# Weight loads moved to the opening and row loads moved back in a fused attention and GLU kernel

## The chip, the core and the metric

The kernel runs on one core of a Trainium2 chip. A core has five instruction streams: TensorE (PE, matrix products; its weight loads are listed as PEld), VectorE (DVE), ScalarE (ACT), GpSimd (POOL) and SyncE (SP, which here only issues transfers). The streams run side by side, each in its own order, and wait for one another through semaphores. The metric is the device time of one execution in microseconds; the time of a kernel is the median of several runs.

## The reference

The program computes a transformer block with adaptive normalisation. A vector c gives six rows of scales and shifts. The first half is attention with a memory, over 2048 tokens in four segments of 512, 32 heads of width 16; the second half is a bilinear GLU.

```python
mod = (silu(c) @ w_mod).reshape(1, 6, 1, -1)
sa, ca, ga, sb, cb, gb = (mod[:, i] for i in range(6))
h = layernorm(x) * (1 + ca) + sa
q, k, v = h @ wq, h @ wk, h @ wv          # 32 heads of 16, 4 segments of 512
for s in range(4):
    p = softmax(qs @ ks.T * scale + mask)  # within the segment
    a_dot = p @ vs
    a_mem = (phi(qs) @ M) / (phi(qs) @ z + 1e-6)
    o = g * a_mem + (1 - g) * a_dot        # g = sigmoid(beta)
    M, z = M + phi(ks).T @ vs, z + phi(ks).sum(0)
x = x + ga * (o @ wo)
h = layernorm(x) * (1 + cb) + sb
x = x + gb * (((h @ w_gate) * (h @ w_up)) @ w_down)
```

phi(t) is t + 1 where t > 0 and exp(t) elsewhere; the mask of the source keeps, for each query, the keys at or after it.

## The kernel before, in words

Heads are worked on in four groups of eight (g = 0 to 3), tokens in segments (s = 0 to 3). Each matrix product in full precision is three products of split operands: high times high, low times high, high times low. A raw weight block is loaded, ACT copies it into the high part, and POOL (or DVE) subtracts to get the low part.

**Opening (L1099 to L1142).** `load_g` (L708) is a generator of two steps: the first takes a staging buffer from the list `stage` (L700) in the order of the calls and issues the load of one group's weights on SP; the second makes ACT's copy (L722) and the subtraction (L723). Weights of groups 0, 1 and 2 are loaded by the opening itself, in that order (`w1`, `w2`); those of group 3 only in `fill_a` (L1003 to L1006), when group 2 begins, with the second step between the keys and the queries of group 2 (L1028). The staging list gives k0, q0 and the first value block the buffers `ph`, then the value blocks `mem`, `pkr`, `f`, then `x` four times, then `mem` twice.

**Projections (`a_kq`, L769).** The keys or the queries of one group and segment are twelve products into one PSUM bank: four blocks of 128 rows of the normalised input (high part `ahH`, low part `ahL`), each in the three forms. For the first keys of segments 1 to 3 a sort (L778) puts all products with `ahH` first and the four with `ahL` behind. ACT copies the bank out (`kf`, `qf`), ACT and POOL split it into three bf16 parts, and SP writes these to DRAM (`kd`, `qd`), from where `load` (L271) brings them into `kst` and `qst`.

**The loop of scores (L1145 to L1203).** It runs over 32 units u, four heads each; u = 8s + 2g + j. In `q_step` PE makes scores by query and DVE takes the row maxima (`nm`); `n_step` transposes those, and a transfer on ACT's queue puts them into two more rows of `qst`. In `k_step` PE makes scores by key and ACT takes the exponential (`pt`), POOL masks it (L341); `av_step` multiplies by v, ACT copies the result (`tsb`) and issues its write `td` on its own queue (L369). Between these steps `fill` draws work from two generators, `fill_a` (projections, memory) and `fill_b` (output projection, the second normalisation, the first gate weights). A number that each step yields decides how much is drawn.

**The tail of the loop (`fill_b`, L1044).** Rows of finished attention output (`orl`) are loaded per segment. Those of segment 2 are loaded when a flag `o0` is set and three segments are done (L1191). `weave(a, b, at)` (L687) puts steps of b at given positions between steps of a; with it the output projection of segment 1 (`wo_mm`) is mixed with `lnC(0)`, which loads the four row blocks `x1_0` of segment 0 and normalises them on DVE, and with `prep(0)` (L435), which loads the first gate and up weights (`w0`), combines them on POOL (L457) and splits them (L448, L452).

**Order of issue.** The rows below show each engine's order as the program fixes it. Every transfer signals on one of eight completion lanes, DMAHW0 to DMAHW7, taken in turn by all transfers of SP and ACT. A transfer waits, before it is issued, until the one that used its lane last has landed; its own lane is the first that its row names. So a transfer issued by ACT can hold ACT for a load that ACT does not need.

Of the kernel before, what the change touches and what calls it, by code (L numbers as in the profile page):

```python
# [20 lines left out]
KT = D // P  # L21
# [37 lines left out]
def tile_kernel(ctx, tc, x, wq, wk_, wv, wo, beta, w_gate, w_up, w_down, c, w_mod, out):  # L59
# [29 lines left out]
    def MM(*a, **k):  # L89
        return pe(nc.tensor.matmul(*a, **k))  # L90
# [19 lines left out]
    def bank(name, dt=F32, shape=(P, 512)):  # L110

        nbank[0] += 1
        return pst(shape, btag[nbank[0] % len(btag)], name, dt)
# [49 lines left out]
    def give():  # L163
        while kept:
            kept.pop(0)()
# [521 lines left out]
    def weave(a, b, at):  # L687

        i = 0
        for w in a:  # L690
            yield w
            if w:
                for _ in range(at.count(i)):
                    w = next(b, None)
                    if w or w is False:
                        yield w
                i += 1

    wH, wL = {}, {}
    stage = [("ph", 3), ("ph", 3), ("ph", 3), ("mem", 2), ("pkr", 1), ("f", 2)] + [("x", 4)] * 4 + [("mem", 2)] * 2  # L700
    nst = [0]

    def staged(nm):
# [65 lines left out]
    def a_kq(s, g, nm):  # L769

        hH, hL = hcur[0]
        ph = phs.setdefault((s, g), {})
        if True:
            dst = kd if nm == "k" else qd
            ps = bank(f"{nm}ps{s}_{g}")
            terms = [(k, a, b) for k in range(KT) for a, b in ((wH, hH), (wL, hH), (wH, hL))]
            if s > 0 and g == 0 and nm == "k":
                terms.sort(key=lambda t: t[2] is hL)  # L778
            for n, (k, a, b) in enumerate(terms):
                MM(ps, a[nm, g][:, k, :], b[k], start=n == 0, stop=n == 11)  # L780
                if n in (2, 5, 8):
                    yield 0.68
            give()
            f = pa.tile([P, L], F32, tag="f", name=f"{nm}f{s}_{g}", bufs=2)
            fast = s == 0 and g == 0
            A, V = (CA, CV) if fast else (act, nc.gpsimd)
            A.activation(f, ps, AF.Copy)
            q3 = pa.tile([P, 3, L], BF, tag="q3", name=f"{nm}3_{s}_{g}", bufs=2)
            r = pa.tile([P, L], F32, tag="qr", name=f"{nm}r_{s}_{g}", bufs=2)

            def part0():
                behind(A.activation(q3[:, 0, :], f, AF.Copy))
                V.tensor_sub(r, f, q3[:, 0, :])

            if fast:
                part0()
            else:
                keep(part0)

            def rest():  # L800
                (CV.tensor_copy if fast else act.copy)(q3[:, 1, :], r)
                V.tensor_sub(q3[:, 2, :], r, q3[:, 1, :])
                for r0, n, k in ((0, 3, 0), (3, 2, 0), (5, 1, 0)) if nm == "k" else ((0, 1, 3), (3, 1, 2), (5, 1, 1)):
                    if nm == "k":
                        nc.sync.dma_start(dst[s][g][r0:r0 + n].rearrange("r p t -> p r t"), q3[:, 0:n, :])
                    else:
                        i = 3 - k
                        nc.sync.dma_start(dst[s][g][r0:r0 + k].rearrange("r p t -> p r t"),
                                          q3[:, i:i + 1, :].to_broadcast([P, k, L]))

            if fast:
                rest()
            phi = (nm == "k" and s < NSEG - 1) or (nm == "q" and s > 0)
            if phi:
                if fast:
                    yield 0.0
                phlog.append((s, g, nm))
                while memq and (s == NSEG - 1 and g > 0 or len(phlog) > 3 and phlog[-4] not in phdone):
                    yield mem_step() or 0.0
                e = pa.tile([P, L], F32, tag="ph", name=f"ph{nm}{s}_{g}", bufs=3)  # L820
                rl = pa.tile([P, L], F32, tag="rl", name=f"rl{nm}{s}_{g}", bufs=1)

                def phi0():
                    behind(act.activation(rl, f, AF.Relu))
                    behind(act.activation(e, f, AF.Exp))

                if fast:
                    phi0()
                else:
                    keep(phi0)  # L830
                ph[nm] = e
            yield 0.68
            if not fast:
                give()
                rest()
            if phi:
                later.append([lambda: pin(vec.scalar_tensor_tensor(e, e, 1.0, rl, op0=ALU.min, op1=ALU.add)), 0, nm])
                if fast:
                    flush("kq")
        nkq[s, g] = nkq.get((s, g), 0) + 1  # L840
        if nkq[s, g] == 2:
            done.add((s, g))
# [97 lines left out]
    B = {"h0": []}  # L940
# [46 lines left out]
    def fill_a():  # L987
# [5 lines left out]
        for s in range(NSEG):  # L993
# [5 lines left out]
            for g in range(2 if s == 0 else 0, NG):  # L999
                ws = []  # L1000
                if s == 0 and g == 2:
                    xts[1] = xload(1)
                if s == 0 and g < 3:  # L1003
                    ws = [load_g(nm, w, g + 1) for nm, w in (("k", wk_), ("q", wq))]
                for w in ws:
                    next(w)  # L1006
                K, Q = a_kq(s, g, "k"), a_kq(s, g, "q")
                if s == 0 and g == 2:
                    lns = a_ln(1)
# [2 lines left out]
                if s < 3 and g > 0:  # L1012
                    p, q = (STEPS0 if s == 0 else STEPS)[g]
# [30 lines left out]
    def fill_b():  # L1044
        open_b()
        pb, bc = B["pb"], B["bc"]
        o1 = wo_load(1, pb, (0, 1))
        xr0 = xr_load(0, pb, (2,))
        o1 += wo_load(1, pb, (2, 3))
        rest = wo_mm(0, us[0], xr0 + xr_load(0, pb, (3,)), (2, 3))  # L1050
        pr = prep(0, "0_0", bc, 1, pb, 1)
        op = wo_op(1, pb, o1, us[1])
        yield from weave(rest, op, (4, 5, 6, 7))
        B["o0"] = True
        lg = lnC(0, pb, bc, pb, "x1", 4)
        rest = weave(wo_mm(1, us[1], xr_load(1, pb, (0,)), pb=pb), chain(op, islice(lg, 10)),
                     (0, 1, 4, 5, 6, 7, 8, 11, 12, 13, 14))
        yield from weave(rest, islice(pr, 1), (10,))
        while "o2" not in B:
            yield None  # L1060
        yield from weave(kept_as("nxt", lg), wo_op(2, pb, B["o2"], us[2]), (0, 1, 2, 3, 3))
        B["orl_free"] = True
        lg = lnC(1, pb, bc, pb, "x1", 4)
        rest = weave(wo_mm(2, us[2], xr_load(2, pb, (0,)), pb=pb), lg, (0, 3, 4, 5, 6, 7, 10, 11, 12, 13))
        yield from weave(rest, pr, (1, 8, 9, 14))
        B["hf"] = yield from lg

    def kept_as(nm, g):
        B[nm] = yield from g
# [47 lines left out]
        pass  # L1117
    next(lw[2])
    next(lw[2])
    w1 = [load_g(nm, w, 1) for nm, w in (("k", wk_), ("q", wq))]  # L1120
    for w in w1:
        next(w)
    run(kq0[1])
    run(kq0[0])
# [111 lines left out]
    hH, hL = B["nxt"]  # L1236
# [94 lines left out]
    for q in range(2):  # L1331
# [62 lines left out]
        for i in range(NF):  # L1394
            g = pre.pop(i + 2) if i + 2 < NF else iter(())
            if i == 0:
                g = chain(pre.pop(1), g)
# [32 lines left out]
        for m in range(2):  # L1430
            s = 2 * q + m
# [111 lines left out]
```

## Time and profile before

| what | us |
|---|---|
| median of 3 runs | 868.59 (866.88 to 870.31) |
| the profiled execution | 865.84 |
| its span on the core | 864.0 |
| opening and first half of the loop, 0 to 430 | 430 |
| end of the loop, 430 to 535 | 105 |
| GLU, 535 to 864 | 329 |

The profile was taken in one execution, and its stamps count from the start of its span. A row of a timeline gives the start, the busy time, the engine, the source line, the operation with output and input, and in brackets how long the engine stood still before it and what ended that. A row of the chain of waits gives start, length and what the end of the program was then waiting for. DMA is the share of the sixteen DMA engines that is busy.

### The profile page before, as it was taken

How to read it: one execution, taken by the hardware profiler on the slowest of the kernel's cores; microseconds unless marked ns; L12 is line 12 of the kernel's file. 1: busy time of each engine (PE TensorE's matmuls, PEld its weight loads, DVE VectorE, ACT ScalarE, POOL GpSimd, SP SyncE). 2: the span in 40 equal slices, each digit the busy share in tenths (PEclk: the TensorE clock that was granted, in tenths of full speed). 3: DMA queues.
4: the chain of work that ended last, by engine and by line, in shares of the span. 5: the costliest groups of instructions: out<-in, count | busy, mean ns of one | idle time of the engine just before them, and what ended most of it. 6: DMA issues, size and time to landing. Idle time of an engine off the chain costs nothing.

```text
span 864.0 us, 14347 instructions
## 1 busy us (share of the span) xinstructions
PE 827.9 (96%) x4823; PEld 580.5 (67%) x4824; DVE 652.1 (75%) x1730; ACT 473.7 (55%) x740; POOL 422.7 (49%) x562
## 2 busy tenths in 40 slices
PE   8979999999999999989997999999999999999998
PEld 5746566556665566555654567888778888887886
DVE  8688678988779777789898878888785667667532
ACT  3747867698668875577545663333364333323321
POOL 4535744577346753586314806998101855550000
PEclk9999999999999999999999999999999999999999
DMA  7773748477566655967894453563315241122032
GB/s 244 233 199 123 229 154 229 151 251 245 159 200 207 214 187 167 271 221 215 253 280 158 148 171 114 168 182 117 107 31 168 74 123 49 50 56 95 0 119 98
DMA packets 111355, 139.45 MB, mean 161 GB/s; under 512 B 18800, under 2 KB 70000, under 8 KB 111280
## 3 DMA queue, kind: packets, MB, share of 16 engines
q1 hardware_dynamic: 106016, 130.91, 49.4%
q10 hardware_dynamic: 5264, 7.62, 2.4%
q8 instruction: 38, 0.62, 0.3%
q14 instruction: 37, 0.30, 0.1%
HBM read 87.48 MB, written 50.76 MB: 160 GB/s over the span
## 4 chain that ended last, share of the span: by engine, by line
PE 70%; DMA 8%; DVE 8%; ACT 6%; POOL 5%; issue 3%; SPq 1%; ACTq 0%; POOLq 0%; DVEq 0%
PE g L90 24%; PE acc L90 14%; PE tb L90 6%; PE k L90 5%; PE q L90 5%; PE vps L90 4%; DVE q L40 3%; PE wops L90 3%; PE kps L90 3%; PE qps L90 3%; ACT pt L338 2%; DMA qd<-q 1%; DMA orl<-od 1%; DMA qst<-nt 1%; DMA memb<-memd 1%
## 5 line engine op out<-in xcount | busy, mean ns | idle before, releaser
L40 DVE CUSTOM_DVE_ANT_0 q<-q,cmask 128x384 f32<-128x384 f32 (+3 forms) x512 | 246.7, 508 | 56.2 <-PE q L90 46.1
L338 ACT ACTIVATE pt<-k 128x1024 f32<-128x1024 f32 x160 | 163.9, 1025 | 66.7 <-PE k L90 54.7
L341 POOL TENSOR_SCALAR_AFFINE_SELECT pt<-pt 128x256 f32<-128x256 f32 (+1 forms) x224 | 106.3, 488 | 143.5 <-ACT pt L338 138.9
L90 PE MATMUL q<-kst,qst 96*128 96x384 bf16 (+3 forms) x512 | 101.3, 300 | 8.4 <-DVE nm L40 7.4
L90 PE MATMUL k<-qst,kst 98*128 98x384 bf16 (+3 forms) x512 | 97.5, 302 | 7.8 <-ACT pt L338 7.3
L457 POOL TENSOR_TENSOR w<-w 128x256 f32<-128x256 f32 (+1 forms) x84 | 72.5, 875 | 65.9 <-DVE t L1228 37.9
L452 POOL TENSOR_TENSOR AL<-w,AH 128x512 fp32r<-128x512 f32 (+1 forms) x42 | 58.8, 1403 | 46.4 <-ACT AH L448 46.4
L90 PE MATMUL tb<-pt,v 128*32 128x512 f32 (+3 forms) x1024 | 75.7, 436 | 0.6 <-POOL pt L341 0.6
L90 PEld LDWEIGHTS <-kst 98*128 98x128 bf16 x512 | 38.2, 99 | 53.1 <-issue 46.0
L40 DVE DVE_READ_ACCUMULATOR2_ANT nm<- 128x1 f32 x512 | 72.1, 141 | 0.0
L448 ACT ACTIVATE AH<-w 128x512 fp32r<-128x512 f32 (+3 forms) x88 | 47.3, 565 | 43.3 <-POOL w L457 30.1
L90 PEld LDWEIGHTS <-qst 96*128 96x128 bf16 x512 | 43.4, 98 | 36.4 <-issue 11.6
L1485 DVE TENSOR_TENSOR mL<-mid,mH 128x512 fp32r<-128x512 f32 (+1 forms) x44 | 32.3, 738 | 41.5 <-ACT mH L1484 41.5
L90 PE MATMUL acc<-DH,mL 128*128 128x512 f32 x144 | 56.6, 393 | 0.9 <-DVE mL L1485 0.9
L90 PE MATMUL acc<-DH,mH 128*128 128x512 f32 x144 | 57.1, 397 | 0.0
L90 PE MATMUL acc<-DL,mH 128*128 128x512 f32 x144 | 56.5, 393 | 0.0
L1484 ACT ACTIVATE mH<-mid 128x512 fp32r<-128x512 f32 (+1 forms) x44 | 27.1, 627 | 51.7 <-PE acc L90 50.5
L90 PEld LDWEIGHTS tb<-pt,v 128*32 128x32 f32 x1024 | 28.6, 109 | 39.3 <-issue 34.5
L1277 ACT ACTIVATE p<-g 128x512 f32<-128x512 f32 (+1 forms) x22 | 13.1, 597 | 74.3 <-PE g L90 74.3
L452 DVE TENSOR_TENSOR AL<-w,AH 128x512 fp32r<-128x512 f32 (+3 forms) x44 | 32.6, 743 | 14.0 <-ACT AH L448 13.9
L367 ACT ACTIVATE tsb<-tb 128x512 f32<-128x512 f32 x32 | 19.1, 596 | 31.8 <-PE tb L90 31.7
L90 PE MATMUL g<-chH,AH 128*128 128x512 f32 (+1 forms) x88 | 34.8, 395 | 0.7 <-ACT p L1277 0.7
(286 smaller groups left out, 2054.6 us busy)
## 6 DMA issues: line engine op xcount, KB each, us to landing
kst<-kd SPq DMA_DIRECT2D x32, 384.0 KB
qst<-qd SPq DMA_DIRECT2D x32, 384.0 KB
td<-tsb ACTq DMA_DIRECT2D x28, 256.0 KB
wm<-in_w_mod_dram SPq DMA_DIRECT2D x24, 256.0 KB
kd<-k SPq DMA_DIRECT2D x16, 384.0 KB
qd<-q SPq DMA_DIRECT2D x16, 384.0 KB
w<-in_w_gate_dram SPq DMA_DIRECT2D x20, 256.0 KB
w<-in_w_up_dram SPq DMA_DIRECT2D x40, 128.0 KB
```

Of the source, the lines that this page charges most:

```text
L40: i = getattr(self.eng, name)(*a, **k)
L90: return pe(nc.tensor.matmul(*a, **k))
L338: lpt[0] = act.activation(pt, kp, AF.Exp, scale=0.25)
L341: sels[u, i] = nc.gpsimd.affine_select(w, w, pattern=[[0, w.shape[1]], [1, P]], compare_op=ALU.is_ge, fill=0.0, base=0, channel_multiplier=-1)
L367: act.activation(tsbs[u], tbs.pop(u), AF.Copy)
L448: i = act.activation(hi[sl], w[sl], AF.Copy)
L452: i = eng.tensor_sub(lo[sl], w[sl], hi[sl].bitcast(F32))
L457: i = ce.tensor_tensor(w[:, o, :, 0:n], w[:, x, :, 0:n], w[:, y, :, 0:n], op=op)
L1277: lcp[0] = act.activation(r["p1"], ps, AF.Copy)
L1484: pin(act.activation(mH[0:n], md[0:n], AF.Copy))
L1485: vec.tensor_sub(mL[0:n], md[0:n], mH[0:n].bitcast(F32))
```

## The change

Four edits. The loads of group 3's raw weights are issued in the opening, right behind those of group 1; their split stays between group 2's keys and queries. The staging list is reordered so that each of them keeps the buffer that it had. The sort of the first keys of segments 1 to 3 now keeps the fourth block's three products together at the end. In `fill_b` the flag `o0` is set later, from a step inside the output projection of segment 1, the steps of `lnC(0)` come up to one position earlier, and the first step of `prep(0)` moves from position 10 to 14; in segment 2's projection one step of `prep(0)` moves from position 1 to 4.

```diff
-    stage = [("ph", 3), ("ph", 3), ("ph", 3), ("mem", 2), ("pkr", 1), ("f", 2)] + [("x", 4)] * 4 + [("mem", 2)] * 2
+    stage = [("ph", 3), ("ph", 3), ("ph", 3), ("mem", 2), ("pkr", 1), ("f", 2)] + [("x", 4)] * 2 + [("mem", 2)] * 2 + [("x", 4)] * 2
...
             if s > 0 and g == 0 and nm == "k":
-                terms.sort(key=lambda t: t[2] is hL)
+                terms.sort(key=lambda t: (t[0] == KT - 1, t[2] is hL))
...
                 if s == 0 and g == 2:
                     xts[1] = xload(1)
-                if s == 0 and g < 3:
-                    ws = [load_g(nm, w, g + 1) for nm, w in (("k", wk_), ("q", wq))]
-                for w in ws:
-                    next(w)
+                    ws = w3
...
         yield from weave(rest, op, (4, 5, 6, 7))
-        B["o0"] = True
         lg = lnC(0, pb, bc, pb, "x1", 4)
         rest = weave(wo_mm(1, us[1], xr_load(1, pb, (0,)), pb=pb), chain(op, islice(lg, 10)),
-                     (0, 1, 4, 5, 6, 7, 8, 11, 12, 13, 14))
-        yield from weave(rest, islice(pr, 1), (10,))
+                     (0, 1, 4, 5, 6, 7, 7, 10, 11, 12, 13))
+        yield from weave(rest, chain(o0_free(), islice(pr, 1)), (8, 14))
...
-        yield from weave(rest, pr, (1, 8, 9, 14))
+        yield from weave(rest, pr, (4, 8, 9, 14))
...
+    def o0_free():
+        B["o0"] = True
+        yield 0.0
...
-    w1 = [load_g(nm, w, 1) for nm, w in (("k", wk_), ("q", wq))]
-    for w in w1:
+    w1, w3 = ([load_g(nm, w, g) for nm, w in (("k", wk_), ("q", wq))] for g in (1, 3))
+    for w in w1 + w3:
         next(w)
```

Three places show how the instructions move. The first is SP's queue in the opening after the change; `wrk` and `wrq` are raw key and query weights with the group's number, `kd0_0` the keys of segment 0 and group 0 on their way to DRAM.

```order
L717 DMA wrk1_491<-in_wk_dram 128x4x128 [waits DMAHW4_49,DVE_49,PE_49]
L717 DMA wrq1_495<-in_wq_dram 128x4x128 [waits DMAHW5_49,DVE_49,PE_49]
L717 DMA wrk3_499<-in_wk_dram 128x4x128 [waits DMAHW6_49]
L717 DMA wrq3_503<-in_wq_dram 128x4x128 [waits DMAHW7_49,DMAHW1_49,DVE_49]
L805 DMA kd0_0_107<-k3_0_0_478 128x512 [waits DMAHW0_49,Activation_49]
```

The two rows of group 3 are new here, at places 22 and 23 of the queue; before, they stood at places 46 and 47, behind the loads of segment 1's input, as these rows of the old order show.

```order
L591 DMA x1_3_688<-in_x_dram 128x512 [waits DMAHW4_49]
L274 DMA qst2_230<-qd0_1_92 96x2048 [waits DMAHW6_49,DMAHW0_49]
L717 DMA wrk3_690<-in_wk_dram 128x4x128
L717 DMA wrq3_694<-in_wq_dram 128x4x128 [waits DMAHW7_49]
L274 DMA kst3_227<-kd0_1_108 96x2048
```

The DVE that `wrq3_503` waits for is the split of the value block that used the buffer `mem` last.

The second place is PE in segment 1, the last six products of the first keys; the names carry segment and block. Before:

```order
L90 MATMUL kps1_0_1172<-ahH1_3_1155,wkH0_316 128x512 [waits Activation_49]
L90 MATMUL kps1_0_1172<-ahH1_3_1155,wkL0_317 128x512
L90 MATMUL kps1_0_1172<-ahL1_0_1014,wkH0_316 128x512 [waits Pool_49]
L90 MATMUL kps1_0_1172<-ahL1_1_1083,wkH0_316 128x512 [waits Pool_49]
L90 MATMUL kps1_0_1172<-ahL1_2_1121,wkH0_316 128x512 [waits Pool_49]
L90 MATMUL kps1_0_1172<-ahL1_3_1156,wkH0_316 128x512 [waits Pool_49]
```

After the change the two products of the fourth block's high part stand behind the low parts of the first three; the last row is the same.

```order
L90 MATMUL kps1_0_1172<-ahL1_0_1014,wkH0_316 128x512 [waits Pool_49]
L90 MATMUL kps1_0_1172<-ahL1_1_1083,wkH0_316 128x512 [waits Pool_49]
L90 MATMUL kps1_0_1172<-ahL1_2_1121,wkH0_316 128x512 [waits Pool_49]
L90 MATMUL kps1_0_1172<-ahH1_3_1155,wkH0_316 128x512 [waits Activation_49]
L90 MATMUL kps1_0_1172<-ahH1_3_1155,wkL0_317 128x512
L90 MATMUL kps1_0_1172<-ahL1_3_1156,wkH0_316 128x512 [waits Pool_49]
```

The third place is SP's queue near the end of the loop. `xr` and `x1_0` are row blocks, `x1d` their copy in DRAM, `memb` a block of memory output, `orl2` the attention rows of segment 2. Before:

```order
L480 DMA orl2_0_5848<-od2_141 128x512 [waits DMAHW1_49,PE_49]
L415 DMA rdd12_183<-rd12_5588 128x2x16 [waits DMAHW2_49,DMAHW0_49,DVE_49]
L480 DMA orl2_1_5850<-od2_141 128x512 [waits DMAHW3_49,PE_49]
L480 DMA orl2_2_5852<-od2_141 128x512 [waits DMAHW4_49,PE_49]
L544 DMA x1d0_3_188<-xr0_3_5634 128x512 [waits DMAHW5_49,DVE_49]
L480 DMA orl2_3_5854<-od2_141 128x512 [waits DMAHW6_49,PE_49]
L274 DMA kst3_227<-kd3_3_122 96x2048 [waits DMAHW7_49,PE_49]
L378 DMA memb12_5888<-memd3_0_135 128x512 [waits DMAHW0_49]
L274 DMA qst3_231<-qd3_3_106 96x2048 [waits DMAHW1_49]
L559 DMA x1_0_3_5862<-x1d0_3_188 128x512 [waits DMAHW5_49,DMAHW2_49]
L530 DMA xr1_3_5892<-in_x_dram 128x512 [waits DMAHW3_49]
```

After the change the four `orl2` rows are gone from here (they stand eleven rows further on, behind `rb12`), `x1_0_3` stands ahead of `memb12`, and `memb12` has gone from lane 0 to lane 5, `x1_0_3` to lane 4.

```order
L415 DMA rdd12_183<-rd12_5588 128x2x16 [waits DMAHW1_49,DMAHW0_49,DVE_49]
L544 DMA x1d0_3_188<-xr0_3_5634 128x512 [waits DMAHW2_49,DVE_49]
L274 DMA kst3_227<-kd3_3_122 96x2048 [waits DMAHW3_49,PE_49]
L559 DMA x1_0_3_5854<-x1d0_3_188 128x512 [waits DMAHW4_49,DMAHW2_49]
L378 DMA memb12_5880<-memd3_0_135 128x512 [waits DMAHW5_49]
L530 DMA xr1_3_5884<-in_x_dram 128x512 [waits DMAHW6_49]
L274 DMA qst3_231<-qd3_3_106 96x2048 [waits DMAHW7_49]
```

This matters to ACT's order, where the write `td27` takes its turn on the lanes. Before, and then after:

```order
L338 ACTIVATE pt28_1_5950<-k28_1_5947 128x1024 [waits PE_49,Pool_49]
L369 DMA td27_170<-tsb27_5938 128x512 [waits DMAHW0_49,Activation_49]
L338 ACTIVATE pt28_2_5982<-k28_2_5977 128x1024 [waits PE_49,Pool_49]
L318 DMA qst1_229<-nt29_5988 2x16x128 [waits DMAHW1_49,DVE_49]
L338 ACTIVATE pt28_3_6029<-k28_3_6024 128x1024 [waits PE_49,Pool_49]
```

```order
L338 ACTIVATE pt28_1_5942<-k28_1_5939 128x1024 [waits PE_49,Pool_49]
L369 DMA td27_170<-tsb27_5930 128x512 [waits DMAHW4_49,Activation_49]
L338 ACTIVATE pt28_2_5974<-k28_2_5969 128x1024 [waits PE_49,Pool_49]
L318 DMA qst1_229<-nt29_5980 2x16x128 [waits DMAHW5_49,DVE_49]
L338 ACTIVATE pt28_3_6021<-k28_3_6016 128x1024 [waits PE_49,Pool_49]
```

`td27` waited for the lane of `memb12` and waits now for that of `x1_0_3`; the small transfer `qst1` waited for that of `qst3` and waits now for that of `memb12`.

## The prediction

> **What bounds the kernel now.** I read the page's busy shares first, then the table by stage, to see where TensorE (PE) has gaps.
>
> ```profile
> span 864.0 us, 14347 instructions
> PE 827.9 (96%) x4823; PEld 580.5 (67%) x4824; DVE 652.1 (75%) x1730; ACT 473.7 (55%) x740; POOL 422.7 (49%) x562
> ```
> ```profile
> 48.00:56.00 8.00, 7.18 (x42) 4.85 (x40) 7.75 (x31) 1.40 (x2) 0.00 (x0) 1.00 1.06 258
> 56.00:64.00 8.00, 4.01 (x23) 2.48 (x22) 6.45 (x24) 6.77 (x11) 6.32 (x5) 0.98 0.32 103
> 64.00:66.00 2.00, 2.00 (x5) 1.01 (x5) 1.14 (x4) 1.78 (x4) 1.82 (x4) 0.50 0.98 345
> 66.00:68.00 2.00, 2.00 (x11) 1.02 (x10) 1.02 (x5) 0.48 (x3) 1.24 (x6) 0.74 0.45 157
> 680.00:730.00 50.00, 50.00 (x219) 40.76 (x218) 33.22 (x42) 16.14 (x31) 30.57 (x31) 1.00 0.32 96
> ```
> The columns of the table are PE, weight load, DVE, ACT, POOL, granted clock, DMA share, GB/s. PE is busy for 96%, and without a gap in the late window shown: the change can only take out gaps (36.1 us in all) or slow-clock time, and whatever it takes out earlier arrives at the end. The deepest hole is 56 to 64, with 4.01 of 8 us busy. The chain of waits names its cause, and ACT's timeline shows it:
>
> ```profile
> 47.24 7.93 DMA wrk<-in_wk_dram
> ```
> ```profile
> 48.41 0.60 ACT L868 ACTIVATE pkr<-mp 128x512 f32<-128x512 f32 x1 [3.16 <-PE mp L93]
> 55.19 1.19 ACT L722 ACTIVATE wkH<-wrk 128x512 fp32r<-128x512 f32 x1 [6.18 <-DMA wrk<-in_wk_dram]
> 57.66 0.63 ACT L787 ACTIVATE kf<-kps 128x512 f32<-128x512 f32 x1
> ```
> The last group's key weights are asked for at 47.24 and land at 55.17. ACT reaches their split at 49.01 and stands still for 6.18 us; everything behind it in ACT's order, the copy kf of group 2's keys first, comes late.
>
> **Part 1, raw weights loaded in the opening.** Two loads of 256 KB move from place 46 of SP's queue to place 22. When ACT comes to the split at 49.0 the data is there.
>
> ```profile
> 51.93 0.40 PE L90 MATMUL kps<-ahL,wkH 128*128 128x512 f32 x1
> 58.35 0.50 PE L90 MATMUL kps<-ahH,wkH 128*128 128x512 f32 x1 [1.46 <-ACT kf L787]
> 61.87 1.19 PE L90 MATMUL mz<-v,pkr 128*128 128x136 f32 x8 [1.67 <-ACT pkr L868]
> 63.93 1.01 PE L90 MATMUL k<-qst,kst 98*128 98x512 bf16 x2 [0.87 <-ACT pt L338]
> ```
> Both splits take 2.47 us (55.19 to 57.66), so ACT would be at kf at 51.5, but its product ends only at 52.33: kf moves from 57.66 to 52.3, by 5.3 us. That is the upper bound. PE's three waits go with it, 4.0 us: the next keys' products follow at once, and the first exponentials can start while PE still works. What is late next is DVE:
>
> ```profile
> 60.03 1.19 DVE L40 SCALAR_TENSOR_TENSOR phk<-phk,rlk 128x512 f32<-128x512 f32 x1 [1.35 <-ACT phk L825]
> 65.40 0.70 DVE L40 CUSTOM_DVE_ANT_0 q<-q,cmask 128x512 f32<-128x512 f32 x1 [0.83 <-PE q L90]
> 67.77 0.21 DVE L40 COPY nt<-ntp 32x128 bf16<-32x128 bf16 x1 [0.96 <-PE ntp L93]
> ```
> Up to 58.6 DVE has work without a pause, and its work does not shrink. It can gain only its three waits, 1.35 + 0.83 + 0.96 = 3.1 us. After 68 it is again nearly full, so its gain is what is passed on. Between DVE's 3.1, PE's 4.0 and kf's 5.3 I take 3.3, nearest to DVE, which paces here. The lower bound is 1.35, if only the first of its waits goes.
>
> On granted clock: the rows above have 0.50 and 0.74 right behind the hole, 2 x 0.50 + 2 x 0.26 = 1.5 us of PE time. The Trainium skill (TensorE: Matmul & The Clock Gate, Part 1: The HAM clock gate) lets the clock fall to half after an idle window of about 3.4 us, and come back after about as much sustained work. Here the longest single wait is 1.67 us and the clock fell all the same, so the row decides. By the rule alone the fall would not be there to be saved; by the row the fuller PE may keep its clock. I leave it out of the sum, since DVE paces that stretch, and make it a rival.
>
> What the move costs where the loads now stand:
>
> ```profile
> 19.50:25.00 5.50, 5.50 (x19) 4.12 (x18) 5.20 (x9) 4.64 (x9) 0.00 (x0) 0.71 0.02 5
> 27.00:39.00 12.00, 11.88 (x52) 9.33 (x50) 5.42 (x6) 9.49 (x14) 8.62 (x6) 1.00 0.91 271
> ```
> ```profile
> 22.80 1.30 DVE L40 TENSOR_TENSOR wvL<-wrv,wvH 128x512 fp32r<-128x512 f32 x2
> ```
> ```profile
> 39.31 0.61 PE L90 MATMUL q<-kst,qst 96*128 96x512 bf16 x2 [0.43 <-DMA qst<-qd]
> ```
> The first of the two loads falls into the DMA engines' empty stretch (share 0.02 from 19.5 to 25). The second reuses the buffer of a value weight and waits on SP until DVE has split it, at 24.10; then the write of the first keys is behind it. At 345 GB/s (the row at 64) 256 KB are 0.76 us, in front of a chain that runs at share 0.91 from 27 to 39 and on which PE waits at 39.31. Bounds 0 and 0.8 us; I take 0.1, because the second load starts where the engines are still empty. **Opening: -3.2 us** (-5.2 to -0.6).
>
> **Part 2, first keys take the fourth block last.** The same twelve products in another order, three times. The waits of PE over the whole run show which of the three had a wait:
>
> ```profile
> PE kps L90 <- ACT ahH L231: 1.2, 1, 1.2
> PE kps L90 <- POOL ahL L232: 0.2, 1, 0.2
> ```
> ```profile
> 88.58 0.50 PE L90 MATMUL kps<-ahH,wkH 128*128 128x512 f32 x1 [1.19 <-ACT ahH L231]
> 90.25 0.50 PE L90 MATMUL kps<-ahL,wkH 128*128 128x512 f32 x1 [0.24 <-POOL ahL L232]
> ```
> Each occurs once, both in segment 1; segments 2 and 3 have nothing to gain. In segment 1 the three products ahead of the late block fill the wait of 1.19 us, but the last product, in both orders, needs the low part of the fourth block, which POOL has ready at 90.25. PE does the work sooner and then waits for the same end. **0 us**; bounds -0.24 and 0.
>
> **Part 3, attention rows and gate weights later (440 to 480).**
>
> ```profile
> 443.54 0.32 SPq L544 DMA_DIRECT2D x1d<-xr  x1
> 446.27 0.42 SPq L378 DMA_DIRECT2D memb<-memd  x1
> 450.14 0.32 SPq L559 DMA_DIRECT2D x<-x1d  x1
> ```
> ```profile
> 446.27 7.61 DMA memb<-memd
> ```
> ```profile
> 454.38 1.02 ACT L338 ACTIVATE pt<-k 128x1024 f32<-128x1024 f32 x1 [3.84 <-DMA memb<-memd]
> ```
> ```profile
> 455.45 0.60 PE L90 MATMUL k<-qst,kst 98*128 98x384 bf16 x4 [1.62 <-ACT pt L338]
> ```
> ```profile
> 455.99 0.69 DVE L40 BATCH_NORM_STATS2 cst<-x 128x6 f32<-128x512 f32 x1 [1.43 <-DMA x<-x1d]
> ```
> ACT has no use for memb: its own write td stands on the same completion lane (the rows of ACT's order) and waits until memb has landed, 7.61 us after its issue. PE loses 1.62 us there and DVE 1.43. In the new order the 1 MB of attention rows is behind all this, about 3 us of the queue at 345 GB/s. But td then stands on the lane of the load x, which waits for the write x1d. In the old trace x1d needed at most 6.6 us (443.54 to 450.14) and x 5.8 (to 455.99). The new x1d goes out about 1.5 us sooner, without the three row loads ahead of it (768 KB, 2.2 us less): landing near 446.4, then x, without the long queue, near 450. ACT comes to td at 450.5, so that the wait is mostly gone: -1.5 (DVE's 1.43 and PE's 1.62 in the same place count once). Bounds -1.6 and +0.7: with both latencies as they were, x would land at 442.0 + 6.6 + 6.0 = 454.6 instead of memb at 453.9.
>
> ```profile
> 469.63 0.33 PE L93 MATMUL ctp<-ident,x 128*128 128x128 f32 x1 [1.36 <-DVE x L40]
> 470.23 0.66 PE L93 MATMUL ctp<-ident,x 128*128 128x128 f32 x4 [0.27 <-DVE xr L40]
> 473.45 0.60 PE L90 MATMUL k<-qst,kst 98*128 98x256 bf16 x4 [1.25 <-ACT pt L338]
> ```
> The row normalisation moves up by one slot on DVE, so the transpose at 469.63 loses its 1.36 us wait. The next one needs DVE's addition, whose end does not move (DVE's total is the same). ACT gets the first column sooner, and the exponential that PE awaits at 473.45 follows about 0.9 us sooner; DVE is full behind it, so I pass on 0.5 (bounds 0 and 1.25).
>
> The gate weights' work on POOL also stands later, now ahead of two masks:
>
> ```profile
> L341 POOL TENSOR_SCALAR_AFFINE_SELECT pt<-pt 128x256 f32<-128x256 f32 (+1 forms) x8 | 5.4, 689 | 1.7 <-ACT pt L338 1.7
> L457 POOL TENSOR_TENSOR w<-w 128x256 f32<-128x256 f32 x4 | 3.8, 949 | 0.0
> L452 POOL TENSOR_TENSOR AL<-w,AH 128x512 fp32r<-128x512 f32 x2 | 2.5, 1268 | 0.0
> ```
> Moved are two w and one AL, 2 x 0.95 + 1.27 = 3.2 us. They leave room before and fill POOL's pauses of 1.7 us after; POOL's total from 476 to 492 is the same, so 0, at most 1.5 late if the masks are short. The rows themselves are needed only where ACT splits them, after 467; asked for near 453, they have 14 us, against a longest load of 7.93 in the rows above. **Tail: -2.0 us** (-2.9 to +2.2).
>
> **Sum.** -3.2 + 0 - 2.0 = -5.2. The profiled execution took 865.84 us (its span and 1.84 around it), so the same would take 860.6. That execution is 2.75 under the median of 868.59; against the median the sum is **863.4 us**.
>
> **Rivals.** *A, a new wait on the lane.* td waits for x as it did for memb: the tail gives +0.7 - 0.5, the whole -3.0, 865.6. For it: x hangs on a write that took up to 6.6 us. Against it: 1 MB is out of the queue. Chance 0.18. *B, the opening's gap reappears.* ACT's splits at 49 and POOL's two subtractions are done, but PE is then held by DVE, and only the first DVE wait, 1.35, goes, less 0.8 for the loads: -0.6 - 2.0 = -2.6, 866.0. For it: DVE is busy for 7.75 of 8 us before 56 (first row of the table by stage). Chance 0.12. *C, slower: SP is held in the opening.* The second weight load waits on SP for DVE's split of a value weight, and the first keys' write is behind it. Every us that it holds beyond 24.3, when the keys are ready, moves PE's 39.31 by one; it decides from a hold of 5.2 us, to 29.5, and at 6 us more gives 869.4. Against it: in the trace DVE is done at 24.10. Chance 0.04. *D, the clock stays up* and PE passes on all of its 1.5 us: 861.9. Chance 0.06.
>
> **How the numbers follow.** The forecast, both gaps closed, has 0.60. About 0.5% (4.3 us, below 864.3) is what a measurement of this kernel tells from no change; of the 0.60, 0.52 lie beyond it, with D 0.58 faster; A, B and the rest 0.38 within; C 0.04. The range is 860.0 to 867.3: the lower end is D with the tail's best, the upper takes in A and B with the spread of the runs (866.88 to 870.31, about 1.7 either way).
>
> **What would show it.** ACT's split of the last keys' weights at about 49 without a DMA wait; kf near 52.3; PE's share in 56 to 64 well over half; DVE's copy nt at 64.6 instead of 67.77; in segment 1 the wait moves from the high to the low part of the fourth block; near 447 no wait of ACT over 1 us. Wrong it would be if ACT's td waits for x, if the first scores of queries come later than 39.3, or if a stage after 70 gives the shift back.

## The result

The changed kernel takes 862.91 us (median of 16 runs, 860.50 to 867.42), the kernel before beside it 867.05 us (16 runs, 863.28 to 870.31): a ratio of 0.9950, with a 95% interval of 0.9931 to 0.9968. That is 4.3 us less by the ratio, a gain of half a per cent, where 5.2 was forecast; the time lies 0.5 us from the forecast of 863.4, which went out from a median of 868.59 in the three runs shown then. Whether it came the way the forecast said is another question, because the profile of the changed kernel is of an execution of 865.02 us, 0.8 us *under* that of before (865.84), not 4 or 5. So one pair of profiles doesn't show where the gain is. That the time came within 0.5 us is in part luck: the forecast went out from a median that the 16 runs put 1.5 us lower, and took about 1 us too much off it, and the two errors went against each other. Two later executions (922.83 us with the keys alone, 1019.05 us with the late part and the keys) ran at a granted clock of 0.847 and 0.752, where all others had 0.98 or more, and stand in no ratio below.

### The profile page after: what moved, and what is told of

Same layout as the page of the kernel before. It is cut to its first block, busy times and chain, and to the rows that moved or that the text cites. A ratio compares the mean times of both kernels' runs of the same rounds, so it can differ in the third digit from the quotient of the medians.

```text
span 863.3 us, 14349 instructions
## 1 busy us (share of the span) xinstructions
PE 828.9 (96%) x4824; PEld 581.3 (67%) x4824; DVE 656.4 (76%) x1730; ACT 474.1 (55%) x740; POOL 420.8 (49%) x562
## 4 chain that ended last, share of the span: by engine, by line
PE 72%; DVE 10%; ACT 6%; DMA 5%; POOL 3%; issue 2%; SPq 1%; ACTq 0%; POOLq 0%; DVEq 0%
PE g L90 24%; PE acc L90 14%; PE tb L90 6%; PE q L90 5%; PE k L90 5%; PE vps L90 4%; DVE q L40 4%; PE qps L90 3%; PE kps L90 3%; PE wops L90 2%; ACT pt L338 2%; PE up L90 1%; PE mz L90 1%; DMA od<-orow 1%; DVE ast L40 1%
## 5 line engine op out<-in xcount | busy, mean ns | idle before, releaser
L452 POOL TENSOR_TENSOR AL<-w,AH 128x512 fp32r<-128x512 f32 (+1 forms) x42 | 56.4, 1345 | 48.3 <-ACT AH L448 48.3
L452 DVE TENSOR_TENSOR AL<-w,AH 128x512 fp32r<-128x512 f32 (+3 forms) x44 | 35.0, 799 | 10.6 <-ACT AH L448 10.5
```

Source lines behind the costliest of these rows:

```text
L452: i = eng.tensor_sub(lo[sl], w[sl], hi[sl].bitcast(F32))
```

## The profile after

The page of the changed kernel, then its table by stage (columns as before: PE, weight load, DVE, ACT, POOL, granted clock with 1.00 as full speed, DMA share, GB/s):

```profile
span 863.3 us, 14349 instructions
PE 828.9 (96%) x4824; PEld 581.3 (67%) x4824; DVE 656.4 (76%) x1730; ACT 474.1 (55%) x740; POOL 420.8 (49%) x562
```
```profile
38.64:42.06 3.42, 1.19 (x7) 0.57 (x6) 0.81 (x2) 1.15 (x2) 2.49 (x3) 1.00 0.96 280
42.06:45.47 3.41, 3.41 (x12) 2.16 (x10) 1.57 (x5) 1.10 (x2) 0.74 (x1) 0.50 0.72 255
...
56.00:64.00 8.00, 7.41 (x42) 4.97 (x41) 7.80 (x25) 6.25 (x10) 5.26 (x5) 1.00 0.49 169
64.00:66.00 2.00, 0.56 (x2) 0.10 (x1) 1.90 (x9) 1.30 (x3) 1.34 (x3) 1.00 0.38 135
66.00:68.00 2.00, 1.64 (x10) 0.95 (x10) 1.97 (x9) 0.07 (x1) 1.15 (x6) 1.00 0.19 66
...
458.48:461.90 3.42, 1.88 (x8) 0.78 (x7) 2.58 (x9) 0.59 (x1) 1.96 (x2) 1.00 0.34 119
461.90:465.31 3.41, 3.03 (x18) 0.87 (x21) 3.34 (x12) 0.44 (x1) 0.48 (x1) 0.50 0.27 93
```
The hole is gone: PE is busy for 7.41 of 8 us between 56 and 64, where it had 4.01, and the clock is 1.00 behind it. DVE now paces that stretch (7.80 of 8, then 1.90 and 1.97 of 2). But two new stretches stand at half clock, at 42.06 and at 461.90, each behind a window in which PE was busy for less than 2 of 3.4 us.

PE's timeline, ACT's and DVE's in the opening:

```profile
41.61 0.62 PE L90 MATMUL q<-kst,qst 96*128 96x512 bf16 x2 [2.23 <-DMA qst<-qd]
...
62.45 0.38 PE L90 MATMUL q<-kst,qst 96*128 96x256 bf16 x2 [0.49 <-DVE nm L40]
...
65.45 0.38 PE L90 MATMUL q<-kst,qst 96*128 96x512 bf16 x1 [1.27 <-DVE nm L40]
```
```profile
52.14 0.60 ACT L868 ACTIVATE pkr<-mp 128x512 f32<-128x512 f32 x1 [3.17 <-PE mp L93]
52.63 1.12 ACT L722 ACTIVATE wkH<-wrk 128x512 fp32r<-128x512 f32 x1
...
56.46 0.60 ACT L787 ACTIVATE kf<-kps 128x512 f32<-128x512 f32 x1 [1.76 <-DVE nm L40]
```
```profile
68.09 0.21 DVE L40 COPY nt<-ntp 32x128 bf16<-32x128 bf16 x1
```
ACT's split of the last keys' weights has no wait left, where it stood still for 6.18 us. Yet the copy nt comes at 68.09, later than before (67.77), because everything came later already at 41.61: PE waits 2.23 us for the first q load (0.43 before) and then runs the half-clock stretch.

The first keys, by the waits of PE over the whole run:

```profile
PE kps L90 <- POOL ahL L232: 0.9, 1, 0.9
...
PE kps L90 <- ACT ahH L231: 0.4, 1, 0.4
```
1.3 us, against 1.4 before: the wait has moved from the high to the low part and keeps its end.

The tail, by the timelines of ACT, PE and DVE:

```profile
450.18 0.33 ACTq L369 DMA_DIRECT2D td<-tsb  x1
452.08 1.02 ACT L338 ACTIVATE pt<-k 128x1024 f32<-128x1024 f32 x1 [1.26 <-PE k L90]
453.05 0.63 ACTq L318 DMA_DIRECT2D qst<-nt  x1
```
```profile
453.97 0.61 PE L90 MATMUL k<-qst,kst 98*128 98x384 bf16 x4
```
```profile
460.61 0.60 PE L90 MATMUL k<-qst,kst 98*128 98x512 bf16 x2 [1.23 <-DMA qst<-nt]
...
471.45 0.66 PE L93 MATMUL ctp<-ident,x 128*128 128x128 f32 x4 [0.87 <-ACT chf L209]
474.21 0.60 PE L90 MATMUL k<-qst,kst 98*128 98x256 bf16 x4 [0.79 <-ACT pt L338]
```
```profile
459.25 0.69 DVE L40 TENSOR_TENSOR orow<-orow,rb 128x512 f32<-128x512 f32 x1 [1.75 <-DMA orl<-od]
```
td goes out at 450.18 instead of 453.95, ACT no longer waits for memb, and PE's wait of 1.62 us is gone. Behind that there are two waits that were not there: PE waits 1.23 us for ACT's load of nt (8 KB, asked for at 453.05), and DVE 1.75 us before the product that reads rb, the broadcast reciprocals (the row names orl, a tile that the product doesn't read; rb had been asked for at 450.64, and the DMA share is 0.91 from 452 to 460). Of the transposes' waits 1.36 and 0.27 us are gone and 0.87 for ACT's chf has come; of the 1.25 behind them 0.46 is gone. That is 1.2 us less waiting.

## How the runs are compared

Each kernel below was timed beside runs of the kernel before on the same chip, and a ratio is against these alone. Beside the time each gave one profile. In a profile I looked up when the same PE instruction starts as in the first profile of before, at eight places, and took the difference from place to place: how much PE lost (+) or gained (-) in that stretch. All kernels but for the key order have PE's instructions in one order, and around a moved row the next one was taken. A star marks a stretch in which the records show half clock for 3.4 us or more. The places are at 36, 53, 91, 445, 455.4, 467, 480 and 540 us of the first profile.

```
kernel           ratio  (95%)          36-53  53-91  91-445 445-455 455-467 467-480 480-540
before, 2nd       -                    +0.62  -0.92* -0.38  -0.43   +3.53*  -0.07   -1.38
keys alone       1.0015 (.9994-1.0035) +0.92  -0.47* +0.04  -1.28   +0.37   -0.06   -1.35
opening alone    0.9985 (.9964-1.0006) +0.74  -2.75* +2.28* -0.63   +3.72*  -0.07   -1.35
opening + keys   1.0001 (.9982-1.0021) +1.12  -3.41  +0.54  +1.50   +1.62*  +1.65*  -1.20
opening + norm   0.9980 (.9956-1.0004) +1.11  -3.41  +0.09  -0.37   +1.52   -1.34   -0.87
late alone       0.9984 (.9960-1.0008) +0.53  -0.05* -0.21  -1.77   +2.67   -1.35   -1.35
late + keys      1.0004 (.9982-1.0026) -0.31  -0.44* +7.86* -1.76   +1.80   -1.34   -0.87
whole, 1st       0.9950 (.9931-.9968)  +3.21* -3.39  -0.04  -1.76   +3.67*  -1.33   -1.25
whole, 2nd       0.9962 (.9944-.9980)  +0.79  -3.40  +0.14  -1.77   +1.81   -1.34   -1.36
opening + late   0.9955 (.9939-.9970)  +1.35  -2.73* +4.70* -1.77   +1.83   -1.34   -1.34
loads behind     0.9949 (.9930-.9968)  +1.17  -3.38  -0.09  -1.76   +1.81   -1.32   -1.32
rows next        0.9935 (.9916-.9954)  +2.68* -3.41  +5.33* -1.78   +1.16   -1.34   -1.03
both repairs     0.9909 (.9881-.9938)  -0.27  -3.39  +1.00  -1.77   +2.04   -1.34   -1.25
```
Read down the columns. Three terms come out the same to 0.1 us: the closed gap (53 to 91, -3.4 in the seven kernels with the opening that have no half-clock stretch there, -2.7 in the two that have one), the lane (445 to 455, -1.77 in all eight with the rows moved) and the normalisation (467 to 480, -1.34 in all nine that have it). These are against one execution of before, and the executions without the edit differ from it too: by 0 to -0.92 in the gap, by -1.28 to +1.50 in the lane. Two columns can't be put down to an edit. From 91 to 445 no instruction moves but for the keys, and four of the changed kernels lose 2.3 to 7.9 us there, with half-clock stretches near 160 and, in three of them, near 382, where PE waits 0.9 us for DVE in before too; the whole change, with all the edits, loses at most 0.1 there in two executions. What starts these losses is open. From 480 to 540 all thirteen others beat the first profile of before by 0.9 to 1.4 us, so that profile had an accident there (its wait of 0.63 us at 504.54, which the second doesn't have). The two that remain, 36 to 53 and 455 to 467, are where gains are lost again.

## Experiments: the parts

The opening alone:

```diff
-    stage = [("ph", 3), ("ph", 3), ("ph", 3), ("mem", 2), ("pkr", 1), ("f", 2)] + [("x", 4)] * 4 + [("mem", 2)] * 2
+    stage = [("ph", 3), ("ph", 3), ("ph", 3), ("mem", 2), ("pkr", 1), ("f", 2)] + [("x", 4)] * 2 + [("mem", 2)] * 2 + [("x", 4)] * 2
...
-                if s == 0 and g < 3:
-                    ws = [load_g(nm, w, g + 1) for nm, w in (("k", wk_), ("q", wq))]
-                for w in ws:
-                    next(w)
+                    ws = w3
...
-    for w in w1:
+    for w in w1 + w3:
         next(w)
```


> Only the change of the opening (order of the raw buffers, last group's two loads in front of the first keys' write). Theory of the prediction: 3.2 us faster than before (2.6 to 4 would bear it out), ACT's split of the last group without a DMA wait, PE's first wait for the q load as before (0.4 us). Rival, read from the profile after the change, where PE waits 2.23 us for the q load at 41.6 and then runs a stretch at half clock: the move only shifts the gap, 0 to 1 us faster, and the q load lands 1.5 to 2.5 us later than before in this profile too.

0.9985: 1.3 us faster by the ratio, between the two theories. In the table the gap is closed (-2.75, and -0.66 more in the kernels where the half-clock stretch near 64 doesn't fall), against a loss of 0.74 before it; the rest of its loss lies where nothing was edited.

The key order alone:

```diff
-                terms.sort(key=lambda t: t[2] is hL)
+                terms.sort(key=lambda t: (t[0] == KT - 1, t[2] is hL))
```


> Only the order of the twelve products of each first key block. Theory of the prediction: 0 us (within 1), the last product waits for POOL's low part at the same place in segment 1, by 0.9 to 1.4 us instead of 0.24, and the wait of 1.19 us for ACT's high part shrinks. Rival: PE hides the 1.2 us and the exponentials behind come sooner, 1 us or more faster.

1.0015, an interval around 1. The whole change without it (below) is as fast as with it. PE's three products at 89.16 start at 87.73, though this execution is 0.5 us late just ahead of them, and the last one, at 90.25 before, starts at 90.78, as late as that. By the waits 0 us stands; the ratio alone would not tell it from a loss of some 2 us.

The late part alone:

```diff
-        B["o0"] = True
...
-                     (0, 1, 4, 5, 6, 7, 8, 11, 12, 13, 14))
-        yield from weave(rest, islice(pr, 1), (10,))
+                     (0, 1, 4, 5, 6, 7, 7, 10, 11, 12, 13))
+        yield from weave(rest, chain(o0_free(), islice(pr, 1)), (8, 14))
...
-        yield from weave(rest, pr, (1, 8, 9, 14))
+        yield from weave(rest, pr, (4, 8, 9, 14))
```


> Only the late part: attention rows of the third row block and gate weights later, row normalisation one slot earlier. Theory of the prediction: 2.0 us faster; ACT issues td without a wait for memb, no ACT wait over 2 us between 447 and 456. Rival, read from the profile after the change: the 1 MB of attention rows now goes out (452 to 455) beside ACT's 8 KB load of nt, which lands only at 460.5, PE waits 1.2 us there and runs 3.4 us at half clock; then 0 to 0.8 us faster.

0.9984, 1.4 us. Both theories were partly right: the lane's 1.77 and the normalisation's 1.35 are there, and 2.67 are lost between them, with PE waiting 0.49 us for nt and 1.31 for DVE.

The whole change once more, with no edit:

> The whole change once more, for a second profile. Both theories: 3 to 5 us faster than before on the median. The prediction's parts would show PE 5 us earlier by 72 us and again 2 us by 480. The rival: PE no earlier than before at 72 us, a wait of 1 us or more for qst on the q load near 41 and on nt near 460, and the difference of the medians comes from fewer half-clock stretches.

0.9962. This execution's span is 858.4 us, 4.9 under that of the first profile of the *same* kernel, and has no half-clock stretch but one at the very end. In the opening it shows what the prediction described:

```profile
39.91 0.61 PE L90 MATMUL q<-kst,qst 96*128 96x512 bf16 x2 [1.21 <-DMA qst<-qd]
```
```profile
53.36 0.60 ACT L787 ACTIVATE kf<-kps 128x512 f32<-128x512 f32 x1 [1.75 <-DVE nm L40]
```
```profile
64.98 0.21 DVE L40 COPY nt<-ntp 32x128 bf16<-32x128 bf16 x1
```
kf at 53.36 (52.3 was said), nt at 64.98 (64.6 was said), PE 2.78 us ahead at 91. It waits 1.21 us for the q load. SP isn't held here: it sends the second early load at 23.88 and the first keys' write at 24.34 (24.32 in before).

The kernel before again, with no edit:

> The kernel before, unchanged, for a second profile: how far do two executions of one program lie apart, and where. Theory of the prediction: the waits it counted are there again (ACT 3 us or more for memb's lane near 454, PE 1 us or more at 455, ACT 5 us or more for the last group's weights near 50). Rival, read from the four changed kernels, which all lack it: the wait of 0.63 us at 504.5 and what follows (1.1 us) was an accident of the first profile and is not there.

867.06 us. ACT's timeline has the two waits again:

```profile
54.84 1.21 ACT L722 ACTIVATE wkH<-wrk 128x512 fp32r<-128x512 f32 x1 [5.02 <-DMA wrk<-in_wk_dram]
```
```profile
453.45 1.02 ACT L338 ACTIVATE pt<-k 128x1024 f32<-128x1024 f32 x1 [3.41 <-DMA memb<-memd]
```
The wait at 504.5 is not there. And this one loses 3.53 us between 455 and 467, which the first profile of before didn't: the old tail has this loss too, and the profile that I predicted from had been spared it.

The change without one of its parts:

```diff
-                terms.sort(key=lambda t: (t[0] == KT - 1, t[2] is hL))
+                terms.sort(key=lambda t: t[2] is hL)
```


> The change without its new order of the first keys' products. Theory of the prediction: as fast as the whole change (864.0 to 862.9, within 0.8), since both orders wait for the same low part. Rival, from the keys alone, whose median lay 2.4 us above that of before: the new order costs 1 to 2 us, and without it the time is 861.5 to 862.5.

0.9955: as fast as the whole change. Next, the late part's lines put back as in the diff above:

> The change without its late part (attention rows and gate weights as before). Theory of the prediction: 3.2 us faster than before (863.8). Rival, from the opening alone (1.3 us faster): 0.5 to 2 us faster (865 to 866.5); the wait of ACT for memb's lane is back (2.5 us or more near 454).

1.0001: no gain at all, under both theories. PE is 2.28 us ahead at 91 and 1.74 at 445, and loses all of it in the old tail. ACT's timeline of this kernel:

```profile
454.14 1.02 ACT L338 ACTIVATE pt<-k 128x1024 f32<-128x1024 f32 x1 [5.34 <-DMA memb<-memd]
```
ACT came earlier and waited longer for memb (5.34 us, 3.84 in before). I took this for the reason why the opening needs the late part; a later kernel speaks against it (below). Last, the opening's lines put back:

> The change without its opening. Theory of the prediction: 2.0 us faster than before (865.0). Rival, from the late part alone (1.1 us faster by the medians): 0 to 1.5 us faster; either way the gap of PE at 58 to 64 and the half-clock stretch near 64 are back, and PE stands at the old place by 72 us.

1.0004. The gap and the stretch near 64 (58.8 here) are back, the lane and the normalisation gain as always, and this execution lost 7.86 us between 91 and 445, where it has no edit but the keys.

## Experiments: lane or normalisation, and two repairs

The kernels of this group keep the old key order. First the opening, and of the late part only the normalisation:

```diff
-                     (0, 1, 4, 5, 6, 7, 8, 11, 12, 13, 14))
+                     (0, 1, 4, 5, 6, 7, 7, 10, 11, 12, 13))
```


> The opening, and of the late part the row normalisation one slot earlier alone: attention rows and gate weights as before, so ACT's write td stands behind memb again. If the late part gains by the moved rows (memb no longer at the end of the DMA queue that td waits for): no faster than the opening alone, 865 to 867.5, ACT waits 2.5 us or more near 454, and PE's waits of 1.3 us at the transpose near 470 and of 1.25 us behind it shrink by up to 0.5 us each. If it gains by the normalisation: 862.5 to 864, with the wait for memb still there.

0.9980. ACT's timeline and PE's:

```profile
451.62 1.02 ACT L338 ACTIVATE pt<-k 128x1024 f32<-128x1024 f32 x1 [3.47 <-DMA memb<-memd]
```
```profile
468.02 0.66 PE L93 MATMUL ctp<-ident,x 128*128 128x128 f32 x4 [0.87 <-ACT chf L209]
```
The two halves come apart: with the rows at their old place the wait for memb is there and the lane's gain is not (-0.37), while the transpose's wait is gone (-1.34). So the lane's 1.77 comes from the moved rows and 1.34 from the normalisation; the gate weights, at their old place here, make no difference to the latter. But this execution loses 1.52 us between 455 and 467 with the rows at their old place, and DVE's timeline there shows why the rows can't be all of it:

```profile
457.22 0.73 DVE L40 TENSOR_TENSOR orow<-orow,rb 128x512 f32<-128x512 f32 x1 [1.37 <-DMA rb<-rdd]
457.87 0.54 DVE L40 TENSOR_SCALAR x<-x,cmv,cy 128x512 f32<-128x512 f32 x1
```
DVE waits for rb, and the row normalisation, moved up, now stands with 0.54 us ahead of maxima that PE waits for. So part of the 1.34 may be paid just ahead of it, and by the ratios (0.9980 here, 0.9985 for the opening alone) the normalisation by itself shows no gain clear of the noise. And memb was through at 451.6 here, 2.5 us sooner than in the kernel without the late part, with PE 0.65 us further ahead at 445: its end does not stand still while PE moves.

The last group's loads behind the second load of the first keys, with the buffers of before:

```diff
-    for w in w1 + w3:
+    for w in w1:
         next(w)
...
     load(1)
     load(2)
+    for w in w3:
+        next(w)
```


> Opening and late part, but the last group's two loads go out behind the second load of the first keys (near 32), in the buffers that they had before, so that SP isn't held for the value weight's split. If the hold pushes the first q load: its landing comes back from 39.9 to 41.6 to 39.3 to 39.9, PE's gap at 58 to 64 is gone all the same, and the time is 0.5 to 1.5 us under the whole change (861.5 to 862.5). If the 512 KB themselves push it: no better than 862.9 to 863.5.

0.9949, no better. PE's timeline:

```profile
41.09 0.61 PE L90 MATMUL q<-kst,qst 96*128 96x512 bf16 x2 [1.60 <-DMA qst<-qd]
```
The value weight's split holds nothing on SP here and the q load is as late as ever. So the 512 KB ahead of it cost this without any hold.

The attention rows one place later on SP, behind the next write of x:

```diff
-        yield from weave(rest, chain(o0_free(), islice(pr, 1)), (8, 14))
+        yield from weave(rest, chain(o0_free(), islice(pr, 1)), (10, 14))
```


> Opening and late part, with the attention rows one place later still (behind the write of the next row of x, near 457). If the 1 MB of rows delays the 8 KB load of nt and the broadcast rb before it: nt lands by 457.5 rather than 459.6 to 460.6, PE has no wait of over 0.2 us for it, the waits for DVE's maxima near 461 (0.75 to 1.31) shrink, and the time is 0.5 to 1.5 us under the whole change. If the queue is full there whatever goes last: no difference (within 0.5).

0.9935. Of PE's waits from 440 to 480 the longest are these, and DVE's product with rb has none:

```profile
PE k L90 <- ACT pt L338: 1.3, 2, 0.8
PE q L90 <- DVE nm L40: 1.1, 3, 0.5
PE ctp L93 <- ACT chf L209: 0.9, 1, 0.9
```
```profile
461.68 0.69 DVE L40 TENSOR_TENSOR orow<-orow,rb 128x512 f32<-128x512 f32 x1
```
The wait for nt is gone and the loss between 455 and 467 is 1.16 us, the least of all kernels with the rows moved. So the 1 MB did delay the 8 KB. For rb the row says less: it was asked for at 454.47 here, 7.2 us ahead of the product. The time is not told apart from the whole change by these intervals.

Both repairs: the rows as in the last kernel, and the last group's loads behind the first two q loads, issued from within the values' products and again with the buffers of before:

```diff
-        yield from av
+        for i, w in enumerate(av):
+            if i == 4:
+                for x in w3:
+                    next(x)
+            yield w
```


> Opening and late part with both repairs: the last group's loads go out behind the first two q loads (near 36.5, between the writes of the second keys), and the attention rows one place later as in the last run. If the traffic ahead of the first q load is what the early loads cost: it lands at 39.2 to 40.1, PE stands 2.5 to 3.5 us earlier than before from 91 us on, and the time is 0.6 to 0.9 per cent under before. If the loads take as much from the writes of the second keys as they gave back: PE 1 to 2 us earlier at 91 us, and 0.4 to 0.6 per cent.

860.43 us, 0.9909 (0.9881 to 0.9938): faster than before by 0.9%, and its interval overlaps that of the whole change only between 0.9931 and 0.9938, and those of its repetition and of the opening with the late part, its parent, not at all. PE's timeline, ACT's and DVE's of this kernel:

```profile
39.16 0.60 PE L90 MATMUL q<-kst,qst 96*128 96x512 bf16 x2 [0.17 <-DMA qst<-qd]
```
```profile
52.60 0.60 ACT L787 ACTIVATE kf<-kps 128x512 f32<-128x512 f32 x1 [1.77 <-DVE nm L40]
```
```profile
64.22 0.21 DVE L40 COPY nt<-ntp 32x128 bf16<-32x128 bf16 x1
```
With nothing ahead of the q load its wait is 0.17 us, kf is at 52.60, nt at 64.22, and PE is 3.55 us ahead at 91. In this execution the opening is worth what its gap is worth, with the loads put where they delay nobody. The tail still loses 2.04, with no wait for nt, and the chain of waits names the transfer that DVE's product ends on:

```profile
448.41 7.69 DMA rb<-rdd
```
The rows go out at 453.75 here, 5.3 us behind rb, and DVE still waits 1.54 us for it.

## Why the prediction was right, and where it was not

**The gap closes, and DVE paces it: right in mechanism, a little too large in size.** The term was 3.3 us, between DVE's three waits and PE's. The nine executions with the opening show -3.25 on average against the first profile of before, but the five without it (that profile among them, as zero) show -0.4, so the opening's part is 2.9. The clock that rival D set apart stayed up in seven of the nine and is inside that number, with 0.66 us and not the 1.5 of the rival.

**"I take 0.1, because the second load starts where the engines are still empty": this step failed.** Seven executions with the early loads lose 0.7 to 3.2 us between 36 and 53, mean 1.6; four without the opening, and the first profile of before as zero, have a mean of 0.35. So the price is about 1.2 us, where the bound from the bytes was 0.8. PE's first wait for q is 1.16 to 2.23 us in the seven and 0 to 1.36 in the five; the 0.43 of the profile that I worked from was among the short ones. In the kernel with both repairs, which has the loads elsewhere, the loss is gone. Where a q load came late enough (2.23 and 1.80 us of waiting), a half-clock stretch came on top; the five without one have a mean of 1.0, a price of 0.7, within the bound. The mechanism of rival C, SP held by the value weight's split, was not needed: the second execution of the whole change had no hold and the kernel that can't have one paid the same.

**Key order, 0: right**, by the waits (1.2 + 0.2 us before, 0.4 + 0.9 after); the ratios don't contradict it.

**The lane: right, -1.6 for -1.5** (-1.77, less the -0.2 that the six executions without the moved rows have on average). Rival A's new wait did not come: td never waited for x in eight executions.

**The normalisation: the wait went as told, the size was wrong.** "DVE is full behind it, so I pass on 0.5": from 467 to 480 it passed on 1.34. But the 0.54 us that it takes on DVE now stand further ahead, in the stretch where the tail loses, so that its net worth may be less.

**"The rows are behind all this" left out who is beside them.** PE waits 0.20 to 1.23 us for nt, mean 0.7, in the six executions with the rows as in the change; 0 to 0.53, mean 0.1, in the six with the rows at their old place; and not at all in the two with the rows later. So the rows cost the load of nt about 0.6 us. No term had this. They are not the whole loss between 455 and 467: the six with the rows as in the change lose 1.8 to 3.7 there, mean 2.3, the six with the rows at their old place 0 to 3.7, mean 1.8. Only 0.5 us of it can be put down to the change. DVE's wait for rb comes with the rows at their old place (1.37) and with the rows later (1.54); why rb lands as late as it does is open. The profile that I worked from had no loss there, so my tail was measured against an execution that was better than usual there and, by 1.2 us, worse than usual after 480.

The sum, each term as the mean with the edit less the mean without: gap -2.9, lane -1.6, normalisation -1.3 (without the one execution that has half clock there), loads +1.2, tail +0.5. That makes -4.1, where I had -5.2 and the medians show -4.1 (the ratio -4.3). Two costs were too small by 1.6 us together, the gap's gain too large by 0.4, the normalisation's too small by 0.8: the total came near because errors cancelled. One figure of the range doesn't follow from its words: D with the tail's best is 861.9 - 0.9 = 861.0, not 860.0.

**What stays open.** By the ratios the opening alone is worth -0.1 and 1.3 us (with and without the keys), the late part alone -0.3 and 1.4, both together 3.3 to 4.3. The intervals, each about 1.8 us to either side, hardly allow a plain sum. In three of the four pairs that differ by the key order alone, the kernel with the new order is 1.3 to 1.7 us slower by the ratios, each within the noise; a small cost of it outside the waits shown is not excluded. By the mean granted clock of the timed runs, (1 - clock) x span / 1.71 us gives the count of half-clock stretches: on average 3.2 in 97 runs of before and 2.1 in 28 of the whole change, but 2.6 and 2.9 with the opening alone and 3.5 and 3.4 with the late part alone. The runs of before alone differ by as much from one group of experiments to the next (2.9 to 4.0). Why the count falls only with both is not settled.

## What to carry to other kernels

A load that is moved ahead is paid for by the transfers behind it in the same stretch, here by 0.7 us and, where PE then stood still long enough to lose its clock, by more than its bytes; put it behind the first transfer that an engine waits for, not just early. When rows are moved out of one wait, look for the small transfers (here 8 KB) that then share the queue with them. And before explaining a difference of half a per cent from two profiles, take a second profile of the unchanged kernel: here two executions of one program lay 4.9 us apart, more than the whole change.

## What the chip showed that I had not expected

About half of the spread between executions goes with a count of half-clock stretches. They are 3.41 us long, or twice that, and within one execution they start whole multiples of that apart: in the table by stage of the changed kernel, from 42.06 to 461.90 are 419.84 us, 123.0 x 3.413. In another execution of the same kernel the grid lies elsewhere and the clock falls only in the last microseconds. Outside the first 20 and the last 10 us, the windows ahead of a stretch had PE busy for 0.4 to 1.95 of 3.41 us (1.19 and 1.88 in the rows above), never more; some windows with 1.6 to 1.95 had no stretch behind them. A line through the runs' times against their counts gives 1.0 us per stretch in before and 1.4 in the changed kernel, and accounts for 0.60 and 0.49 of the variance.

The Trainium skill (TensorE: Matmul & The Clock Gate, Part 1: The HAM clock gate) has a free-running window of 3413 ns that doesn't reset when a kernel starts; the traces agree. Its rule that the clock falls after an idle window of about 3.4 us is too narrow here: a window that was half busy was enough, as the one ahead of 461.90, whose longest single wait is the 1.23 us for nt.

The second thing is the completion lane: an engine that issues a DMA waited 2.55 to 5.34 us for a transfer that it has no use for, in all six executions where td and memb share a lane, and in none of the eight where they don't.
